# Sigmoid attention with a mixture-of-depths layer: the routed rows as Strassen products of quarters

## Chip, core and metric

The kernel runs on one core of a Trainium2 chip, as one launch, from inputs in DRAM to an output in DRAM. The metric is the device time of the launch in microseconds (us). All arithmetic is in fp32.

## The reference, cut to what matters

```python
# attention: q, k, v are (8, 12, 448, 64)
scores = scale * np.matmul(q, k.transpose(0, 1, 3, 2)) - np.log(S)
attn = 1.0 / (1.0 + np.exp(-scores))
x = np.matmul(attn, v)              # then (B, H, S, D) -> (B, S, H*D): (8, 448, 768)

# mixture of depths: w_gate (768), w1 (768, 1024), w2 (1024, 768), capacity 128
scores = np.einsum('bsd,d->bs', x, w_gate)
out = x.copy()
for b in range(B):
    top_idx = np.argpartition(-scores[b], capacity)[:capacity]
    xe = x[b, top_idx]
    h = np.maximum(xe @ w1, 0.0)
    ye = h @ w2
    g = 1.0 / (1.0 + np.exp(-scores[b, top_idx]))
    out[b, top_idx] = x[b, top_idx] + g[:, None] * ye
```

So each of the 8 sequences sends 128 of its 448 rows through two weight matrices.

## The kernel before, in words

**Attention.** The 96 heads are handled in 24 groups of four (`load`, `turn`), two groups in each of 12 stages s. A stage has seven units n = 0 to 6 (`unit`): 32 score matmuls on TensorE (L213) into two PSUM tiles `psc`, then two sigmoids on ScalarE (L221). `turn(i)` (L188 to L195) transposes the raw q and k rows of group i on VectorE into `qT` and `kT`; groups 2s and 2s+1 are used in stage s, unit 3 needs both. The values of stage s (`values`, L248) are multiplied after unit 6 of stage s and after units 0, 1 and 2 of stage s+1; they fill the PSUM tiles `o`, which four transposes (`take`, L263) empty into `x_b`.

**Loads.** All plain loads and stores stand on the queue of SyncE (SP), in the order of the code: `load` (q and k rows, two buffers each), `load_v` (eight transfers, two buffers), the weight matrices once, near the end of stages 0 and 1, into tiles that stay in SBUF. `store` writes x_b to a DRAM tile `x_d` in four transfers of 128-byte pieces, `copy_out` copies `x_d` to the output.

**Routing.** When a sequence's x is complete, `gate` (DVE) makes its scores; `spread` sends them to DRAM and back as a row on each partition (`rep`), `rank` and `place` count for each row how many are larger, `choose` turns that into 128 row numbers and gathers the rows from `x_d` (GpSimd queue). These steps are `put` at fixed places (stage, unit) and run after the unit by `due`. The small transfers of routing stand on the queue of GpSimd (POOL).

**The routed rows.** `turn_rows` transposes the 128 gathered rows on TensorE (L375). `ffn1` multiplies weights by rows, three blocks of 128 outputs at a time (L391, relu by ScalarE, L394). `ffn2` (L401) multiplies the hidden rows by a third of the second matrix, DVE scales by the gate and adds to the rows (L403), and an indirect DMA scatters them into the output. These pieces wait in the list `ready`; `go` takes one after each of units 3, 4 and 5 from stage 4 on, and the rest after the last stage. They use the tiles `o`, in turn with `psc` at the end.

The order on every engine is the order of the code (`tc.manual_schedule()`); a tile pool makes a new tile wait until the old one in its buffer has been read.

## Time and profile before

| | |
|---|---|
| runs | 472.99 us median of 3 (472.17 to 476.65) |
| profiled execution, its own time | 476.17 us |
| span of the profile | 474.4 us, mean granted clock 0.991 |
| TensorE (PE) busy | 457.4 us (96%) |
| DVE, ACT, POOL busy | 227.3, 184.9, 48.8 us |
| scores L213, values L248 (raw_v), busy | 153.9, 142.2 us |
| routed L391 (tiles o), L401 (tiles o and psc), busy | 69.8, 62.5 and 25.4 us |
| DMA | 72.74 MB, mean 153 GB/s |

In the profile's groups a line such as "L391 PE MATMUL o<-xeT,w_sb ... x576 | 69.8, 281 | ..." reads: line of the kernel, engine, operation, output and inputs, number of instructions, busy time in us, mean ns of one, idle time ahead of it and what ended that. An fp32 matmul is two instructions. The chain of work is followed back from the last instruction; its pieces are start, length and what ran. SPq is SP's queue of DMA issues, raw_k, raw_q and raw_v the tiles of the loads, w_sb both weight matrices. Busy matmuls overlap, so their busy time is not a sum of work.

### The profile page before, as it was taken

To read this page: it belongs to the slowest core of one execution; us is meant where nothing else is said; L and a number is where in the kernel's file an instruction comes from. 1 tells how busy PE (TensorE), PEld (TensorE's weight loads), DVE (VectorE), ACT (ScalarE), POOL (GpSimd) and SP (SyncE) were. 2 spreads that over 40 slices of the span, in tenths; PEclk is the share of its full clock that TensorE was granted. 3 is DMA by queue.
4 is the path that set the end of the run, shared out by engine and by line. 5 is a ranking of instruction groups with operands and counts; after the bars stand their busy time and mean duration, and the time that the engine had idled before them with its cause. 6 is when DMAs were issued, how large, how long until landed. Compare 5 with 4: busy or idle time off the path is not lost.

```text
span 474.4 us, 14579 instructions
## 1 busy us (share of the span) xinstructions
PE 457.4 (96%) x6582; PEld 312.6 (66%) x6582; DVE 227.3 (48%) x559; ACT 184.9 (39%) x245; POOL 48.8 (10%) x76
## 2 busy tenths in 40 slices
PE   8998989897999999999999999999999999999994
PEld 3563635365765684658774666755678738999993
DVE  4309087749140825765710864946254618530100
ACT  4756464544235334435445334445344420101000
POOL 9000000110000011011100011011010010220001
PEclk9999999999899999999999999999999999999999
DMA  8988788799921980985940992985822734722000
GB/s 268 229 324 212 291 196 178 158 262 195 227 70 45 202 202 8 229 177 149 258 171 3 202 202 43 266 153 130 254 69 43 155 83 79 209 57 68 35 0 33
DMA packets 119005, 72.74 MB, mean 153 GB/s; under 512 B 96320, under 2 KB 108800, under 8 KB 118688
## 3 DMA queue, kind: packets, MB, share of 16 engines
q1 hardware_dynamic: 115808, 61.35, 50.8%
q0 software_dynamic: 3136, 10.47, 10.0%
q8 instruction: 51, 0.84, 0.7%
q14 instruction: 10, 0.08, 0.0%
HBM read 57.51 MB, written 25.31 MB: 175 GB/s over the span
## 4 chain that ended last, share of the span: by engine, by line
PE 89%; DMA 4%; DVE 2%; ACT 1%; issue 1%; SPq 0%; POOLq 0%; DVEq 0%; ACTq 0%
PE o L248 25%; PE psc L213 24%; PE o L391 16%; PE o L401 13%; PE psc L401 4%; PE psc L391 3%; PE o L213 2%; DMA raw_h<-in_v_dram 1%; ACT attn L221 1%; DMA scores<-total 1%; DMA rep<-scores 1%; PE o L375 1%; PE o L506 1%; DVE scr L321 1%; DVE scr L318 1%
## 5 line engine op out<-in xcount | busy, mean ns | idle before, releaser
L221 ACT ACTIVATE attn<-psc,bias_s 128x896 f32<-128x896 f32 x156 | 148.6, 1004 | 121.0 <-PE psc L213 120.8
L213 PE MATMUL psc<-qT,kT 32*64 32x448 f32 x2496 | 153.9, 542 | 4.2 <-ACT attn L221 4.2
L248 PE MATMUL o<-attn,raw_v 32*64 32x448 f32 x2304 | 142.2, 540 | 1.1 <-ACT o L251 1.1
L213 PEld LDWEIGHTS psc<-qT,kT 32*64 32x64 f32 x2496 | 66.4, 131 | 57.6 <-issue 33.9
L248 PEld LDWEIGHTS o<-attn,raw_v 32*64 32x64 f32 x2304 | 70.2, 133 | 46.3 <-issue 33.4
L391 PEld LDWEIGHTS o<-xeT,w_sb 128*128 128x128 f32 x576 | 67.2, 196 | 9.8 <-issue 5.7
L263 DVE STREAM_TRANSPOSE x_b<-o 128x448 f32<-128x448 f32 x48 | 26.9, 617 | 97.1 <-PE o L248 97.0
L391 PE MATMUL o<-xeT,w_sb 128*128 128x128 f32 x576 | 69.8, 281 | 0.9 <-ACT xeT L381 0.9
L401 PE MATMUL o<-w_sb,hT 128*128 128x256 f32 x272 | 62.5, 383 | 0.0
L401 PEld LDWEIGHTS o<-w_sb,hT 128*128 128x128 f32 x272 | 50.5, 190 | 14.2 <-issue 4.3
L188 DVE STREAM_TRANSPOSE kT<-raw_k 128x384 f32<-128x384 f32 x48 | 24.7, 552 | 34.2 <-PE psc L213 27.5
L403 DVE SCALAR_TENSOR_TENSOR xe<-o,gate,xe 128x256 f32<-128x256 f32 x17 | 8.2, 483 | 53.4 <-PE o L401 53.3
L318 DVE TENSOR_SCALAR_CACHE_REDUCE scr<-rep,score 128x448 f32<-128x448 f32 (+1 forms) x32 | 21.5, 673 | 20.1 <-DMA rep<-scores 19.2
L274 DVE TENSOR_REDUCE gate_p<-scr 128x14 f32<-128x448 f32 x48 | 29.8, 621 | 1.7
L271 DVE TENSOR_TENSOR scr<-x_b,wg_b 128x448 f32<-128x448 f32 x48 | 29.4, 613 | 1.1
L248 PE MATMUL o<-attn,raw_h 32*64 32x448 f32 x384 | 28.8, 536 | 0.0
L394 ACT ACTIVATE hT<-o 128x384 f32<-128x384 f32 (+1 forms) x20 | 9.1, 453 | 49.5 <-PE o L391 49.5
L401 PE MATMUL psc<-w_sb,hT 128*128 128x256 f32 x112 | 25.4, 380 | 0.0
L195 DVE STREAM_TRANSPOSE qT<-raw_q 128x896 f32<-128x896 f32 x23 | 24.7, 1073 | 1.4 <-DMA raw_q<-in_q_dram 1.4
L401 PEld LDWEIGHTS psc<-w_sb,hT 128*128 128x128 f32 x112 | 21.0, 190 | 3.4 <-issue 0.7
L321 DVE SCALAR_TENSOR_TENSOR scr<-rep,score,earlier 128x448 f32<-128x448 f32 (+1 forms) x32 | 21.8, 683 | 1.4
L298 POOL DMA_DIRECT2D scores<-total x8 | 4.4, 555 | 173.5 <-DVE by_token L300 165.3
(69 smaller groups left out, 222.7 us busy)
## 6 DMA issues: line engine op xcount, KB each, us to landing
raw_k<-in_k_dram SPq DMA_DIRECT2D x24, 448.0 KB, 5.1
raw_q<-in_q_dram SPq DMA_DIRECT2D x24, 448.0 KB, 4.7
x_d<-x_b SPq DMA_DIRECT2D x32, 336.0 KB, 7.6
out_dram<-x_d SPq DMA_DIRECT2D x8, 1344.0 KB, 8.5
raw_v<-in_v_dram SPq DMA_DIRECT2D x48, 192.0 KB, 4.4
w_sb<-in_moe_w_dram SPq DMA_DIRECT2D x6, 512.0 KB, 5.7
w_sb<-in_moe_w_dram SPq DMA_DIRECT2D x8, 384.0 KB, 9.0
spot<-ranks POOLq DMA_DIRECT2D x8, 256.0 KB, 6.2
```

What stands on the lines that cost most here:

```text
L188: nc.vector.transpose(kT[i][:, e, :HK], sk[:, e, :HK].rearrange("p (m c) d -> p c m d", c=NF))
L195: nc.vector.transpose(qT[i], sq)
L213: nc.tensor.matmul(psc[h // 2][y * Dh:(y + 1) * Dh, h % 2, :S], kT[2 * s + x][d, e, r:r + 2, :].rearrange("d r t -> d (r t)"), qT[2 * s + ...
L221: nc.scalar.activation(a, psc[pr][:, :, :S], AF.Sigmoid, bias=bias_s, scale=QK_SCALE)
L248: nc.tensor.matmul(o[x][j * Dh:(j + 1) * Dh, pr, :S], w, a[rows, j, :], start=(n == 0 and c == 0), stop=(n == 3 and c == NF - 1))
L263: nc.vector.transpose(x_tiles[b][:, :, 2 * g + pr, :], outs[s][x][:, pr, :S].rearrange("p (r t) -> p r t", t=TT))
L271: nc.vector.tensor_tensor(out=tmp, in0=x_tiles[b][:, :, hp, :], in1=wg_b[:, hp:hp + 1, :].to_broadcast([P, TB, TT]), op=ALU.mult)
L274: nc.vector.tensor_reduce(out=gate_parts[b][:, :, hp], in_=tmp, axis=AX.X, op=ALU.add)
L318: nc.vector.tensor_scalar(out=junk[:n], in0=rep[:n], scalar1=own, scalar2=0.0, op0=ALU.is_gt, op1=ALU.add, accum_out=above[:n, c:c + 1])
L321: nc.vector.scalar_tensor_tensor(out=junk[:n], in0=rep[:n], scalar=own, in1=earlier[:n, c, :], op0=ALU.is_equal, op1=ALU.mult, accum_out=l ...
L391: nc.tensor.matmul(ps[:, f - f0, :n], w1_sb[:, t, f * P:(f + 1) * P], xeT[:, t // (KD // 2), t % (KD // 2), :n], start=(t == 0), stop=(t = ...
L401: nc.tensor.matmul(ps[:n, :ND], st[b]["hT"][:, t, :n], w2_sb[:, t, cols], start=(t == 0), stop=(t == KF - 1))
```

## The change

Two sequences make a pair; their rows together are a matrix of two row halves, and each weight matrix is cut into quarters. Seven products of quarters by sums of halves take the place of eight (Strassen's scheme in the form with shared sums). For the first matrix, products 1, 2 and 4 use quarters as they are, 3, 5, 6 and 7 use sums of quarters; for the second, 1, 2 and 3 use quarters, 4, 5, 6 and 7 sums.

- `load_weights` loads the quarters; GpSimd makes the eight sums, which are stored in DRAM.
- Three quarters of each matrix stay in SBUF. A sum is loaded when needed (`lend`, on SP) into two attention tiles that are free at that time: after unit 2 of a stage by the table `LENT`, later in `rest`.
- `turn_rows` makes the differences of rows (on DVE for pairs 0 and 3, GpSimd otherwise), `first` and `second` make a product of 12 and 4 matmuls in half of a PSUM tile, `first_sums` and `second_sums` add the products on DVE (and on GpSimd for differences of hidden rows).
- Where each product runs is written out in `WORK` (stage, unit) and `rest`; `ready` and `go` are gone.
- `raw` and `vals` have one buffer. `load(2s+2)` now follows `turn(2s+1)`, `load(2s+3)` follows `turn(2s+2)` at the end of a stage, and `load_v(s)` stands after unit 3 of its own stage. Attention tiles have fixed slots.
- For sequences 2 to 6 the small transfers of routing move from POOL's queue to SP's (`queue`), ahead of the x_d stores; copies to the output move (`routed`).

The core of the diff:

```diff
-    raw = ctx.enter_context(tc.tile_pool(name="raw", bufs=2))
-    vals = ctx.enter_context(tc.tile_pool(name="vals", bufs=2))
+    raw = ctx.enter_context(tc.tile_pool(name="raw", bufs=1))
+    vals = ctx.enter_context(tc.tile_pool(name="vals", bufs=1))
     head = ctx.enter_context(tc.tile_pool(name="head", bufs=2))
-    dram = ctx.enter_context(tc.tile_pool(name="dram", bufs=3, space=bass.MemoryType.DRAM))
+    dram = ctx.enter_context(tc.tile_pool(name="dram", bufs=B, space=bass.MemoryType.DRAM))
...
-        raws[i] = [raw.tile([P, TB * Dh], F32, name=f"raw_{nm}") for nm in "kq"]
+        if i == 1:
+            both = moe.tile([P, 7 * KH * P], F32, name="rows_t")
+            raws[i] = [both[:, n * TB * Dh:(n + 1) * TB * Dh] for n in range(2)]
+        else:
+            raws[i] = [raw.tile([P, TB * Dh], F32, name=f"raw_{nm}") for nm in "kq"]
...
+    def load_weights(m):
+        n = KH if m == 1 else FH
+        w = (w1_sb, w2_sb)[m - 1]
+        held = [(0, 0), (0, 1), (1, 1)] if m == 1 else [(0, 0), (1, 0), (1, 1)]
+        left = (1, 0) if m == 1 else (0, 1)
+        room = moe.tile([P, 7 * FH * P], F32, name="hidden")
+        a, b = room[:, :QW], room[:, QW:2 * QW]
+        c = moe.tile([P, 7 * KH * P], F32, name="rows_t")[:, :QW]
+        for dst, at in [(a, left)] + [(w[:, x], held[x]) for x in (2, 0, 1)]:
+            nc.sync.dma_start(out=dst.rearrange("p (t c) -> p t c", t=n), in_=quarter(m, *at))
+        w00, wx, w11 = [w[:, x] for x in range(3)]
+        def made(key, src):
+            t = sums[m, key] = dram.tile([P, QW], F32, name=f"sum{m}{key}", bufs=1)
+            nc.gpsimd.dma_start(out=t, in_=src)
+        if m == 1:
+            ops = [(5, b, a, w11, ALU.add), (6, c, b, w00, ALU.subtract),
+                   (7, a, w00, a, ALU.subtract), (3, b, wx, c, ALU.subtract)]
+        else:
+            ops = [(5, b, a, w00, ALU.subtract), (6, c, w11, b, ALU.subtract),
+                   (7, a, a, w11, ALU.subtract), (4, b, wx, c, ALU.subtract)]
+        for key, dst, x, y, op in ops:
+            nc.gpsimd.tensor_tensor(out=dst, in0=x, in1=y, op=op)
+            made(key, dst)
+    def attn_tile(pr, slot):
+        return attnp.tile([P, 2, S], F32, name=f"attn{pr}_{slot}")
+    def lend(m, key, slot):
+        halves = []
+        for pr in range(2):
+            t = attn_tile(pr, slot).rearrange("p a s -> p (a s)")[:, :QW // 2]
+            nc.sync.dma_start(out=t, in_=sums[m, key][:, pr * QW // 2:(pr + 1) * QW // 2])
+            halves.append(t)
+        lent[m, key] = halves
...
+            a = attn_tile(pr, f"d{s % 2}{n}" if n < 3 else f"u{n}")
...
+    def queue(b):
+        return nc.gpsimd if b < 2 or b == B - 1 else nc.sync
...
+        nc.scalar.activation(x[:, 2, :, :n], ps[:, 0, :KH, :n], AF.Copy)
+        nc.vector.tensor_copy(x[:, 3, :, :n], ps[:, 1, :KH, :n])
+        eng = nc.vector if p in (0, NP - 1) else nc.gpsimd
+        for dst, y, z in ((4, 2, 0), (2, 3, 2), (5, 3, 4), (6, 1, 5)):
+            eng.tensor_tensor(out=x[:, dst, :, :n], in0=x[:, y, :, :n], in1=x[:, z, :, :n],
+                              op=ALU.subtract)
...
+    ROWS1 = {1: 0, 2: 1, 3: 3, 4: 6, 5: 4, 6: 5, 7: 2}
+    def first(p, key, where="o"):
+        n = CAP
+        x = pairs[p]["x"][:, ROWS1[key]]
+        if key == 1:
+            t = moe.tile([P, 7 * FH * P], F32, name="hidden")
+            pairs[p]["h"] = t.rearrange("p (m k n) -> p m k n", m=7, k=FH)
+        w = weight(1, key)
+        ps = bank(where).rearrange("p (k n) -> p k n", n=P)
+        for f in range(FH):
+            for t in range(KH):
+                nc.tensor.matmul(ps[:, f, :n], w((t * FH + f) * P, P), x[:, t, :n],
+                                 start=(t == 0), stop=(t == KH - 1))
+        return p, key, ps
...
+    def first_sums(p, key, ps):
+        n = CAP
+        h = [pairs[p]["h"][:, m, :, :n] for m in range(7)]
+        ps = ps[:, :FH, :n]
+        def add(dst, a, b):
+            nc.vector.tensor_tensor(out=dst, in0=a, in1=b, op=ALU.add)
+        def relu(t):
+            nc.scalar.activation(t, t, AF.Relu)
+        if key == 1:
+            nc.scalar.activation(h[2], ps, AF.Copy)
+        elif key == 2:
+            add(h[0], ps, h[2])
+            relu(h[0])
+        elif key == 6:
+            add(h[2], ps, h[2])
...
+            if p == NP - 1:
+                nc.vector.scalar_tensor_tensor(out=h[4], in0=h[2], scalar=0.0, in1=h[3],
+                                               op0=ALU.max, op1=ALU.add)
+                nc.vector.tensor_tensor(out=h[5], in0=h[4], in1=h[0], op=ALU.subtract)
+                nc.vector.scalar_tensor_tensor(out=h[2], in0=h[2], scalar=0.0, in1=h[0],
+                                               op0=ALU.max, op1=ALU.subtract)
+                nc.vector.tensor_tensor(out=h[6], in0=h[1], in1=h[5], op=ALU.subtract)
+                return
+            relu(h[2])
+            for dst, a, b, op in ((4, 2, 3, ALU.add), (5, 4, 0, ALU.subtract),
+                                  (2, 2, 0, ALU.subtract), (6, 1, 5, ALU.subtract)):
+                nc.gpsimd.tensor_tensor(out=h[dst], in0=h[a], in1=h[b], op=op)
...
+    ROWS2 = {1: 0, 2: 1, 3: 6, 4: 3, 5: 4, 6: 5, 7: 2}
+    QUARTERS = {1: ((0, 0), (0, 1), (1, 0), (1, 1)), 2: ((0, 0),), 3: ((0, 1),), 4: ((1, 0),),
+                5: ((1, 1), (0, 1)), 6: ((0, 1), (1, 0), (1, 1)), 7: ((1, 1), (1, 0))}
+    def second(p, key, where="o"):
+        n = CAP
+        h = pairs[p]["h"][:, ROWS2[key]]
+        w = weight(2, key)
+        ps = bank(where)
+        for t in range(FH):
+            nc.tensor.matmul(ps[:n, :DH], h[:, t, :n], w(t * DH, DH),
+                             start=(t == 0), stop=(t == FH - 1))
+        return p, key, ps
+    def second_sums(p, key, ps):
+        n = CAP
+        left = pairs[p].setdefault("left", {q: 4 if q[0] or q[1] else 2 for q in QUARTERS[1]})
+        for x, m in QUARTERS[key]:
+            b = 2 * p + x
+            cols = slice(m * DH, (m + 1) * DH)
+            xe = st[b]["xe"]
+            nc.vector.scalar_tensor_tensor(
+                out=xe[:n, cols], in0=ps[:n, :DH], scalar=st[b]["gate"][:n, 0:1],
+                in1=xe[:n, cols], op0=ALU.mult, op1=ALU.add)
+            left[x, m] -= 1
+            if p == NP - 1 and not left[x, m]:
+                scatter(b, m)
...
+    WORK = {
+        (4, 3): [("t", 0)], (4, 4): [(1, 0, 1)], (4, 5): [(1, 0, 2)],
+        (5, 3): [("t", 1)], (5, 4): [(1, 0, 7), (1, 0, 6)], (5, 5): [(1, 0, 4)],
+        (6, 3): [(2, 0, 1), (2, 0, 2)], (6, 4): [(1, 0, 5)], (6, 5): [(1, 0, 3), (2, 0, 4)],
+        (7, 3): [(2, 0, 3)], (7, 4): [(2, 0, 5)], (7, 5): [(2, 0, 6), (2, 0, 7), ("s", 0)],
+        (8, 3): [("t", 2), ("t", 3), (1, 1, 1)], (8, 4): [(1, 1, 2)],
+        (8, 5): [(1, 1, 7), (1, 1, 6)],
+        (9, 3): [(1, 1, 4)], (9, 4): [(1, 1, 5)], (9, 5): [(1, 1, 3), (2, 1, 1)],
+        (10, 3): [(2, 1, 2)], (10, 4): [(2, 1, 4), (2, 1, 5)], (10, 5): [(2, 1, 6)],
+        (11, 3): [(2, 1, 3)], (11, 4): [(2, 1, 7), ("s", 1)],
+        (11, 5): [("t", 4), ("t", 5), (1, 2, 1), (1, 2, 2)],
+    }
+    LENT = {5: [(1, 7), (1, 6)], 6: [(1, 5), (1, 3), (2, 4)], 7: [(2, 5), (2, 6), (2, 7)],
+            8: [(1, 7), (1, 6)], 9: [(1, 5), (1, 3)], 10: [(2, 4), (2, 5), (2, 6)],
+            11: [(2, 7), (1, 7), (1, 6)]}
...
+        put(s, 4, spread, b)
+        put(s, 4, store, b)
+        put(s + 1, 1, ranking, b)
         if s + 2 <= NS:
-            put(late, *((s + 1, 6) if b == 0 else (s + 2, 0)), choose, b)
-            put(late, s + 2, 3, follow, b)
+            put(*((s + 2, 1) if b % 2 else (s + 1, 5)), copy_out, b)
+            put(s + 2, 0, choose, b)
...
+                for i, (m, key) in enumerate(LENT.get(s, ())):
+                    lend(m, key, f"d{(s + 1) % 2}{i}")
...
+    def rest():
+        for n in range(3):
+            gap(NS, n)
+        room = [f"d1{i}" for i in range(3)] + [f"u{n}" for n in range(3, NU)] + ["d00"]
+        for key in ((1, 5), (1, 3)):
+            lend(*key, room.pop(0))
+        p, b = NP - 2, B - 1
+        work = [(item, begin(item, "any")) for item in ((1, p, 6), (1, p, 7))]
+        gates(2 * NS - 1)
+        st[b]["x_d"] = None
+        store(b)
+        gate(waiting.pop())
+        for key in ((2, 4), (2, 5), (2, 6), (2, 7), (1, 7)):
+            lend(*key, room.pop(0))
+        for item, args in work:
+            finish(item, args)
+        spread(b)
+        for key in (4, 5, 3):
+            do((1, p, key), "any")
+        lend(1, 6, "d01")
+        ranking(b)
+        choose(b - 1)
+        for key in (1, 2, 3, 4, 5, 6):
+            do((2, p, key), "any")
+        for key, slot in (((1, 5), "d02"), ((1, 3), "d10")):
+            lend(*key, slot)
+        choose(b)
+        do((2, p, 7), "any")
+        do(("s", p))
+        copy_out(b - 1)
+        copy_out(b)
+        p += 1
+        for item in (("t", b - 1), (1, p, 1), (1, p, 2), ("t", b)):
+            do(item, "any")
+        for key, slot in (((2, 6), "d11"), ((2, 5), "d12"), ((2, 7), "u3"), ((2, 4), "u4")):
+            lend(*key, slot)
+        for key in (7, 6, 4, 5, 3):
+            do((1, p, key), "any")
+        for key in (1, 2, 6, 5, 7, 3, 4):
+            do((2, p, key), "any")
...
                     turn(2 * s + 1)
-                    load(2 * s + 3)
-                if n == 0:
-                    load_v(s + 1)
+                    if s > 0:
+                        load(2 * s + 2)
+                if n == 3 and s > 0:
+                    load_v(s)
                 gap(s, n)
                 if n == NU - 2:
                     turn(2 * s + 2)
-                    load(2 * s + 4)
-                load_weights(*WEIGHTS.get((s, n), (0, 0)))
-        for n in range(5):
-            gap(NS, n)
-        go("any")
-        choose(B - 2)
-        while len(ready) > 3:
-            go("any")
-        ranking(B - 1)
-        copy_out(B - 1)
-        while len(ready) > 1:
-            go("any")
-        follow(B - 2, "any")
-        for n in range(2):
-            go("any")
-        choose(B - 1)
-        while len(ready) > 1:
-            go("any")
-        follow(B - 1, "any")
-        while ready:
-            go("any")
-        assert not late
+                    load(2 * s + 3)
+                if n == NU - 2 and s < 2:
+                    load_weights(s + 1)
```

## The prediction, made before the changed kernel was run

> **What bounds the kernel now.** I read the page first: engines, the chain that ended last, the costliest groups.
>
> ```profile
> span 474.4 us, 14579 instructions
> ...
> PE 457.4 (96%) x6582; PEld 312.6 (66%) x6582; DVE 227.3 (48%) x559; ACT 184.9 (39%) x245; POOL 48.8 (10%) x76
> ...
> DMA  8988788799921980985940992985822734722000
> ...
> PE 89%; DMA 4%; DVE 2%; ACT 1%; issue 1%; SPq 0%; POOLq 0%; DVEq 0%; ACTq 0%
> ...
> L391 PE MATMUL o<-xeT,w_sb 128*128 128x128 f32 x576 | 69.8, 281 | 0.9 <-ACT xeT L381 0.9
> ...
> L401 PE MATMUL o<-w_sb,hT 128*128 128x256 f32 x272 | 62.5, 383 | 0.0
> ```
>
> PE is 89% of the chain, so PE work removed counts, as long as nothing new makes PE wait. The routed products (L391, L401) are on that chain. DMA works in bursts: nine tenths in many slices, nothing in others.
>
> Next the chain in order of time, one stage of the attention loop (the values of s=8 end at 294.3; I call that moment T9, and so on):
>
> ```profile
> 295.86 4.25 PE o L391 x36
> 300.12 1.69 PE psc L213 x32
> 301.80 4.22 PE o L391 x36
> 306.02 1.69 PE psc L213 x32
> 307.71 2.88 PE o L391 x24
> ```
>
> 36 matmuls take 4.22, 24 take 2.88; on L401, 16 take 3.65. T9 to T10 (327.3) is 33.0, of which routed work is 11.35: 21.7 is left for scores and values. Then SP's timeline from the same moment, and DVE's ranking:
>
> ```profile
> 299.52 0.38 SPq L95 DMA_DIRECT2D raw_k<-in_k_dram  x1
> ...
> 300.46 0.53 SPq L283 DMA_DIRECT2D out_dram<-x_d  x1
> 301.18 16.71 SPq L280 DMA_DIRECT2D x_d<-x_b  x4
> 317.98 2.76 SPq L95 DMA_DIRECT2D raw_k<-in_k_dram  x1
> 320.84 0.38 SPq L95 DMA_DIRECT2D raw_q<-in_q_dram  x1
> ```
>
> ```profile
> 281.87 0.64 DVE L318 TENSOR_SCALAR_CACHE_REDUCE scr<-rep,score 128x448 f32<-128x448 f32 x1
> ...
> 287.81 0.21 DVE L329 STREAM_TRANSPOSE by_col<-place_s 128x32 f32<-128x32 f32 x1
> ```
>
> The four stores of x_d hold SP's queue for 16.7, because it fills and drains in order: the q and k rows behind them are issued at 318 and 320.8 and land at about 324.7 (4.6 median for raw_q), 30.4 after T9. Here that costs nothing: they are for the transposes near the end of the next stage. The waits of DVE say so:
>
> ```profile
> DVE kT L188 <- DMA raw_k<-in_k_dram: 3.1, 2, 2.7
> ...
> DVE qT L195 <- DMA raw_q<-in_q_dram: 1.4, 2, 0.7
> ```
>
> **The change, part by part.**
>
> *Products.* Each pair has 7 first products of 24 instructions (12 matmuls, two passes) and 7 second ones of 8 with 384 columns; four pairs make 28 and 28, instead of 768 and 384 instructions. A first one is the 24-group above, 2.88 (2.68 in the tail); a second one is 3.65 x 8/16 x 384/256 = 2.74 (2.60). Inside the loop the table of work has 16 first, 14 second and six row transposes of 0.66: 46.1 + 38.4 + 4 = 88.4. Before, from T4 (110.8, plus 3.7 of waiting on DVE) to the end of the values at 392.2, eight intervals less 8 x 21.7 leave about 104. Gain: 15.7.
>
> *The tail.* Before, PE runs from 392.2 to 467.4 without a gap: 75.2. After it has 12 x 2.68 + 14 x 2.60 + 1.3 = 69.9. But the last pair needs both sequences chosen before its third product, and the chain of the last sequence (scores out, rep back, ranking, spot, gather) lies as before: rep at +17.6, ranking to +24, spot landing about +33, gather about +40. I count 0.5 of waiting at the first gather, 2.4 after the second one for its copies and differences, 1.8 for GpSimd's four hidden sums before product 3, so PE ends at about +75.4. Nothing is gained; bounds -5 (no wait) to +4.
>
> *Additions on DVE and ACT.* 8 additions of 512 columns and 14 of 384 per pair, at the rates of L271 (613 ns for 448) and L403 (483 for 256): about 14 per pair, 56 in all, less 11.6 for the old L403. DVE rises to some 280 of 500: room. Cover: PE has four o banks as halves, and the sums trail a product by 0.7 to 1.4. Without cover it is up to 0.7 per product; I take 0.
>
> *Sums of weights on GpSimd.* Eight operations of 1536 columns. Nearest rows: 553 ns for a cast of 448 (1.9 scaled) and 1395 for L172 (4.8). With w1 landed near 28 and stores between, w2 can load from 41 to 52, and the scores of sequence 0, queued on POOL behind them, leave between 60 and 82; rep is back 8 later, ranking needs it at 80. Cost 0 to 10; I take 2, in between.
> The Trainium skill (GPSIMD Engine Reference, section 3.1) gives 4497 ns for a two-input add of 2048 columns; an estimate by it is 3.4 each, and the sum would be 0 for this term.
>
> *Weights from DRAM.* 32 loans of 786 KB. Packets of 3072 bytes (the second matrix's load) took 132 ns on 16 queues: 2.1 per loan, 67 in all, and 18 for the stores of sums. Engines were 61% busy, 292; they come to 377. As a mean that fits; the order on SP doesn't.
>
> *One buffer for q/k rows and v.* This decides. The load for transpose 2s+3 now stands behind turn(2s+2), at the end of stage s, so on SP behind: loans, v, scores, rep (which waits for scores to land), four x_d stores and in stages 6 and 9 a copy to out as well. In the next stage's order on DVE, turn(2s+3) comes before the ranking, and that before the four transposes that free the o banks. So a late row makes PE wait at unit 3 (kT) or at the first routed product (o).
> Row first: with two buffers DVE waited 4.5 in all for these rows. The Trainium skill (Trainium Kernel Development and Optimization, Best Practices) asks for double buffering so that DMA overlaps compute, which speaks against this part; taken with the row of before, the term would be nothing, taken with the rule, what follows.
>
> From T: a loan 2.1, v 4.8 (SP's 8 issues at 260.8 to 264.5 landed at 266.6), scores landing +2, rep +0.7; from the x_d issue to the rows' landing 16.9 (301.18 to 324.7 is 23.5, less 2.9 for rows and 3.7 for the copy ahead); a copy 3.7. After landing: turn 2.2, ranking 5.9 to 6.2, two transposes 1.1; PE can cover 1.7 of that with unit 3.
>
> - Stages 5 and 8 (two loans): landing at T+30.5. T6 is T5+33.5 (21.7 + 9.3 + 2.5), T9 is T8+35. Waits 4.7 and 3.2: take 5 and 3.
> - Stage 6 (three loans, which now leave only after the ranking's ranks and spot, at +8, packets from +11): v has landed at +23, landing of rows 46; stage length 41: 12.9. Stage 9: 42 against 38.8: 10.9. Take 13 and 11.
> - Stage 3 (no loans, scores on POOL, a copy): 26.5 against 26, so ranking ends 6 later than at 113.3. Take 6.
>
> Sum 38. Best case, loans and v leaving at T with no push by the ranking: 3.6 + 2.1 + 7.7 + 7.7 + 3 = 24. Worst, with late loans in full: 54.
> Small ones: stages 4 and 5 have only a transpose between two units, ACT needs 1.9 for a unit's two tiles: 1.3 each, 2.6. In stages 7, 9, 10 the second item needs a loan that comes up to 3.5 late (0 to 3.5 each); I take 4 together.
>
> Sum against the profiled span: 474.4 - 15.7 + 0.2 + 2 + 38 + 2.6 + 4 = 505.5. Its own time was 476.17, 1.8 above the span: 507.3. The median of the runs (472.99) is 0.67% lower: 504.
>
> **Rivals.**
> *The rows come in time* (faster). If x_d, copy and rows drained side by side, so that rows land 7.7 before T (turn and ranking done by then), only the products count: 474.4 - 15.5 = 458.9, or 457.5 by the median. For: DMA stands at 0 in 5 of 40 slices, PE's interval of 33 to 36 is about what SP's chain takes. Against: 16.7 in one SP row, and the order on DVE. It decides from a total of waits under 15.5.
> *Only the bare wait* (slower, small): loans leave at T, waits 24 and no small ones: 483 span, 481 by the median. For: PE's own stretching gives SP time. Against: ranks and spot stand ahead of the loans.
> *Everything late* (slower, large): 54 for the rows and loans, GpSimd's upper end of 10: 523 span, 521. For: one late stage pushes the next. Against: stages 8 and 11 have no ranking and let SP catch up.
> That the products aren't fewer is excluded: the program's order has 56 products.
>
> **How the numbers follow.** Rows late, 504: 0.60, own range 490 to 515. Bare wait 0.12; everything late 0.10; rows in time 0.14; 0.04 near no change, where part of the waits cancels the gain. The range goes from 474, which leaves out rows in time and part of no change, to 524. A change under 1% can't be told from none here. Faster 0.14, same 0.04, slower 0.82.
>
> **What would show it.** Right: DVE's waits for raw_k and raw_q of tens of us, in stages 4, 6, 7, 9, 10, PE's idle time ahead of L213 and of the first routed product, x_d stores on SP followed by rows that land after T; routed products at 2.9 and 2.7; GpSimd sums between 1.9 and 4.8. Wrong: PE busy at 9 in all slices with a span near 460, rows landing before the values end; or waits at the loans (PE waiting for the lent tiles), not at the rows.

## Result and profile after

| | before | after |
|---|---|---|
| median of the runs | 474.82 us (472.17 to 478.45, 4 runs) | 552.68 us (551.53 to 556.21, 4 runs) |
| profiled execution, span, mean granted clock | 476.17, 474.4, 0.991 | 556.21, 554.2, 0.944 |
| T12 (end of the values of the last stage) | 392.2 | 445.9 |
| from T12 to the last matmul | 75.1 | 101.6 |
| PE without work before its last matmul | 8.5 | 80.5 |

After is 1.163 times before (95% interval 1.154 to 1.173). Medians here and below are over all executions, while a ratio and its interval leave out the few that were in a slower state of the chip. The forecast was 504, range 474 to 524: the direction was right, the size was not. The page of after, its head and two groups:

```profile
span 554.2 us, 14369 instructions
...
PE 465.5 (84%) x6326; PEld 273.7 (49%) x6326; DVE 293.8 (53%) x637; ACT 184.6 (33%) x240; POOL 92.5 (17%) x92
...
PEclk9999987896999988997999998998999997799998
...
L533 PE MATMUL o<-w_sb,hidden 128*128 128x384 f32 x72 | 34.9, 645 | 25.9 <-DVE x_b L319 15.6
...
L474 PE MATMUL o<-rows_t,attn_d 128*128 128x128 f32 x264 | 36.0, 300 | 10.2 <-DVE hidden L484 5.7
```

The routed products now stand behind 26 and 10 us of idle time. PE was 0.9 idle ahead of L391 before and not at all ahead of L401 in `o`. PEclk falls to 6 and 7 in slices where PE waits. The list of waits (engine, line, waited for: us in total, times, longest) names four sorts:

```profile
DVE kT L244 <- DMA raw_k<-in_k_dram: 44.2, 9, 12.9
...
PE o L533 <- DVE x_b L319: 15.6, 3, 5.6
PE o L533 <- DVE xe L544: 13.4, 5, 6.3
...
PE psc L269 <- DVE qT L251: 12.9, 4, 9.2
```

The first two are the late rows that the prediction spoke of: DVE's wait for raw_k is 44.2 instead of 3.1. SP's timeline and DVE's around T10 (368.0) show the steps in the order in which they were forecast:

```profile
346.09 9.03 SPq L336 DMA_DIRECT2D x_d<-x_b  x4
355.16 2.95 SPq L339 DMA_DIRECT2D out_dram<-x_d  x1
358.20 1.45 SPq L100 DMA_DIRECT2D raw_k<-in_k_dram  x1
```

```profile
366.57 1.04 DVE L244 STREAM_TRANSPOSE kT<-raw_k 128x384 f32<-128x384 f32 x2 [10.41 <-PE o L304]
...
374.83 2.24 DVE L319 STREAM_TRANSPOSE x_b<-o 128x448 f32<-128x448 f32 x4
```

x_d, the copy, the rows; then on DVE the turn of the rows, the ranking (368.7 to 374.8), and only then the transposes that free `o`. The view puts DVE's 10.41 down to PE, but raw_k landed at 366.5 (358.20 plus 8.3 from issue to landing), 0.1 ahead of the turn. So this wait too is one for late rows, and the 44.2 is a lower bound. PE's first routed product of stage 10 waits 5.6.

The other two sorts were not in the prediction. The 9.2 is the wait of unit 0 of stage 3 for `qT`. PE waits from 74.0 to 83.1. Here is what DVE does ahead of the turn that makes this `qT`, and GpSimd beside it:

```profile
65.07 3.65 DVE L327 TENSOR_TENSOR scr<-x_b,wg_b 128x448 f32<-128x448 f32 x1
68.75 0.62 DVE L330 TENSOR_REDUCE gate_p<-scr 128x14 f32<-128x448 f32 x1
...
70.00 6.92 DVE L353 COPY parts<-by_dim 32x32 f32<-32x32 f32 x4
```

```profile
64.78 3.45 POOL L166 TENSOR_TENSOR rows_t<-w_sb,hidden 128x1536 f32<-128x1536 f32 x1
...
69.10 3.45 POOL L166 TENSOR_TENSOR hidden<-hidden,w_sb 128x1536 f32<-128x1536 f32 x1
...
73.44 3.43 POOL L166 TENSOR_TENSOR hidden<-w_sb,rows_t 128x1536 f32<-128x1536 f32 x1
```

While GpSimd makes the second matrix's sums, a product on DVE that takes 0.58 to 0.63 with no sum beside it takes 3.65, and four small copies that take 0.72 take 6.92. The reduction between them keeps its 0.62.

The last sort is in the tail: second products of pair 2, and what DVE does just ahead of the one that comes late.

```profile
470.57 2.74 PE L533 MATMUL o<-w_sb,hidden 128*128 128x384 f32 x8
479.63 4.18 PE L533 MATMUL o<-w_sb,hidden 128*128 128x384 f32 x6 [6.32 <-DVE xe L544]
```

```profile
476.77 2.18 DVE L544 SCALAR_TENSOR_TENSOR xe<-psc,gate,xe 128x384 f32<-128x384 f32 x4
478.87 0.61 DVE L544 SCALAR_TENSOR_TENSOR xe<-o,gate,xe 128x384 f32<-128x384 f32 x1
```

The product at 479.63 goes into the free half of a tile `o`. It starts 0.15 after DVE has read the product in the other half (478.87 plus 0.61), and that reading stood behind the ranking. GpSimd's last hidden sum had ended at 475.2. So by the trace this product waited for the reader of the other half of its PSUM tile, not for its inputs; the run with a tile for each product tests that.

### The profile page after: what moved, and what is told of

It reads as the page before. It is cut to its first block, busy times and chain, and to the rows that moved or that the text cites. A ratio compares the mean times of both kernels' runs of the same rounds, so it can differ in the third digit from the quotient of the medians.

```text
span 554.2 us, 14369 instructions
## 1 busy us (share of the span) xinstructions
PE 465.5 (84%) x6326; PEld 273.7 (49%) x6326; DVE 293.8 (53%) x637; ACT 184.6 (33%) x240; POOL 92.5 (17%) x92
## 5 line engine op out<-in xcount | busy, mean ns | idle before, releaser
L269 PE MATMUL psc<-qT,kT 32*64 32x448 f32 x2496 | 161.0, 553 | 17.3 <-DVE qT L251 12.9
L304 PE MATMUL o<-attn_d,raw_v 32*64 32x448 f32 x1152 | 131.1, 541 | 0.6 <-ACT o L307 0.3
L304 PE MATMUL o<-attn_u,raw_v 32*64 32x448 f32 x1152 | 127.0, 540 | 1.4 <-ACT o L307 0.8
L277 ACT ACTIVATE attn_u<-psc,bias_s 128x896 f32<-128x896 f32 x86 | 81.9, 1004 | 121.4 <-PE psc L269 121.3
L277 ACT ACTIVATE attn_d<-psc,bias_s 128x896 f32<-128x896 f32 x70 | 66.7, 1004 | 57.8 <-PE psc L269 57.7
L304 PEld LDWEIGHTS o<-attn_u,raw_v 32*64 32x64 f32 x1152 | 51.3, 133 | 30.4 <-issue 21.0
L244 DVE STREAM_TRANSPOSE kT<-raw_k 128x384 f32<-128x384 f32 x46 | 23.8, 555 | 73.6 <-DMA raw_k<-in_k_dram 44.2
L304 PEld LDWEIGHTS o<-attn_d,raw_v 32*64 32x64 f32 x1152 | 50.2, 133 | 21.2 <-issue 18.9
L533 PE MATMUL o<-w_sb,hidden 128*128 128x384 f32 x72 | 34.9, 645 | 25.9 <-DVE x_b L319 15.6
L474 PE MATMUL o<-rows_t,attn_d 128*128 128x128 f32 x264 | 36.0, 300 | 10.2 <-DVE hidden L484 5.7
L474 PEld LDWEIGHTS o<-rows_t,attn_d 128*128 128x128 f32 x264 | 34.2, 213 | 15.0 <-DVE hidden L484 6.7
L533 PEld LDWEIGHTS o<-w_sb,hidden 128*128 128x128 f32 x72 | 17.3, 251 | 42.2 <-issue 34.1
L327 DVE TENSOR_TENSOR scr<-x_b,wg_b 128x448 f32<-128x448 f32 x48 | 36.5, 761 | 1.0
L474 PE MATMUL o<-rows_t,w_sb 128*128 128x128 f32 x264 | 32.3, 279 | 3.4 <-ACT rows_t L451 1.9
L474 PEld LDWEIGHTS o<-rows_t,w_sb 128*128 128x128 f32 x264 | 30.3, 192 | 8.2 <-issue 3.1
```

Of the source, the lines that this page charges most:

```text
L244: nc.vector.transpose(kT[i][:, e, :HK], sk[:, e, :HK].rearrange("p (m c) d -> p c m d", c=NF))
L269: nc.tensor.matmul(psc[h // 2][y * Dh:(y + 1) * Dh, h % 2, :S], kT[2 * s + x][d, e, r:r + 2, :].rearrange("d r t -> d (r t)"), qT[2 * s + ...
L277: nc.scalar.activation(a, psc[pr][:, :, :S], AF.Sigmoid, bias=bias_s, scale=QK_SCALE)
L304: nc.tensor.matmul(o[x][j * Dh:(j + 1) * Dh, pr, :S], w, a[rows, j, :], start=(n == 0 and c == 0), stop=(n == 3 and c == NF - 1))
L327: nc.vector.tensor_tensor(out=tmp, in0=x_tiles[b][:, :, hp, :], in1=wg_b[:, hp:hp + 1, :].to_broadcast([P, TB, TT]), op=ALU.mult)
L474: nc.tensor.matmul(ps[:, f, :n], w((t * FH + f) * P, P), x[:, t, :n], start=(t == 0), stop=(t == KH - 1))
```

## Experiments

Each kernel was timed beside the kernel before on the same chip; T12 and "tail" (T12 to the last matmul) are from the profiled execution. Diffs are against after unless said.

**One part alone.**

*The stores of x_d two units later.*
```diff
-        put(s, 4, store, b)
+        put(s, 6, store, b)
...
-            put(*((s + 2, 1) if b % 2 else (s + 1, 5)), copy_out, b)
+            put(*((s + 2, 1) if b % 2 else (s + 1, 6)), copy_out, b)
```


> Theory A (the rows are late because they stand behind the four x_d stores on SP): with the stores and the copy moved two units later, behind the loads of rows, PE's waits at the first routed product in stages 4, 6, 7 and 10 (5.1, 4.4, 5.6 and 5.6 us, together 20.7) go, and with them the half-clock stretches that follow them (some 10 us); DVE's wait for raw_k falls from 44.2 to under 10. I expect 520 to 535 us against 552.7. Rival B (the DMA engines are full anyway, whatever the order on SP): the rows land as late as now, 545 to 556. Both: the waits of the tail stay, and the wait of 9.2 in stage 3 stays.

556.46, ratio 1.166 (1.150 to 1.181): no gain. DVE's wait for raw_k did fall, from 44.2 to 24.8, but now the loans stand behind the stores: PE waits 9.8, 11.0 and 6.8 for `attn_d<-sum`, where it waited 3.3 and 3.2 in all. Rival B's time, for a reason that neither theory named: a wait changes its place when SP's order does.

*A PSUM tile for each product.*
```diff
-        if half[0] is None:
-            half[0] = banks(where)
-            return half[0][:, 0]
-        t, half[0] = half[0], None
-        return t[:, 1]
+        return banks(where)[:, 0]
```


> Each product gets a PSUM tile of its own instead of half of one. Theory A (a product in the second half of a tile waits until DVE has read the first half's product, because the wait is made for the tile): the waits at tiles read by the sums, 4.8, 6.3, 1.8, 1.2 and a dozen of 0.7 to 0.9 in the tail and 2.3, 1.8 in the loop, together about 22, shrink, and the half-clock stretches of the tail with them: 530 to 540 us. Rival B (the sums stand on DVE behind gates and ranking, and the products need them as inputs or for the buffer anyway): the waits move to other products, 545 to 556.

539.65, 1.130 (1.115 to 1.145). As theory A has it: 13 less; the tail goes from 101.6 to 88.2. Of the tail's 10.0 of idle time that is left, the longest piece (3.6) is ahead of the transposes of sequence 6's rows.

*The small sums on DVE.*
```diff
-        eng = nc.vector if p in (0, NP - 1) else nc.gpsimd
+        eng = nc.vector
...
-                nc.gpsimd.tensor_tensor(out=h[dst], in0=h[a], in1=h[b], op=op)
+                nc.vector.tensor_tensor(out=h[dst], in0=h[a], in1=h[b], op=op)
```


> The row differences of pairs 1 and 2 and the hidden sums of pairs 0 to 2 made on DVE instead of GpSimd; the eight sums of weights stay on GpSimd. Theory A (only the long sums of weights matter, the small ones lie beside other work): 548 to 557 us. Rival B (every two-input operation of GpSimd holds DVE up, and the small ones too): DVE's sums behind them get shorter and the time falls by about 10, 540 to 545.

556.57, 1.171 (1.162 to 1.179). Theory A.

*No sums of weights.*
```diff
-            nc.gpsimd.tensor_tensor(out=dst, in0=x, in1=y, op=op)
-            made(key, dst)
+            made(key, a)
```


> Leaves out the eight additions of weight quarters on GpSimd: a plain quarter is stored in DRAM in place of each sum, with the same transfers, so the products use other weights. Theory A (while GpSimd adds two tiles, DVE stands still: the copies of L353 took 6.9 instead of 0.7 us and one operation of L327 3.65 instead of 0.6): the turn of stage 3's rows comes in time, the wait of 9.2 ahead of unit 3 of stage 3 goes and so does most of the 10.2 us at half clock behind it: 537 to 543 us. Rival B (the rows of that stage are late through the transfers of the sums and of x_d): the wait stays within 2 us of 9.2, 549 to 556.

550.19, 1.155 (1.144 to 1.167): rival B's range, and the 2.5 less than after are within the intervals. (The text says unit 3 of stage 3; the wait is ahead of unit 0 of that stage.) DVE's copies and products are back:

```profile
66.18 0.63 DVE L326 TENSOR_TENSOR scr<-x_b,wg_b 128x448 f32<-128x448 f32 x1
...
68.09 0.72 DVE L352 COPY parts<-by_dim 32x32 f32<-32x32 f32 x4
```

The 9.2 is gone and T2 to T3 takes 27.6 instead of 37.1. But T3 to T4 takes 35.7 instead of 27.9, with PE waiting 1.9 for the turn and 4.2 for x_b, after DVE has waited 15.6 for raw_k: the chain of late rows, a stage earlier. So the mechanism of theory A is shown, and its price is not: 7.8 of the 9.5 are given back in the next stage.

*Sums of weights in eight pieces.* (`QW` is 1536.)
```diff
-            nc.gpsimd.tensor_tensor(out=dst, in0=x, in1=y, op=op)
+            for o in range(0, QW, QW // 8):
+                nc.gpsimd.tensor_tensor(out=dst[:, o:o + QW // 8], in0=x[:, o:o + QW // 8],
+                                        in1=y[:, o:o + QW // 8], op=op)
```


> Each sum of weights on GpSimd is made in eight pieces of 192 columns instead of one operation of 1536. Theory A (DVE is held for as long as one GpSimd operation lasts): DVE's copies of L353 and the operations of L327 wait at most 0.5 us each, the turn for stage 3 comes in time and the wait of 9.2 shrinks to under 3; a part comes back in stage 4, as without the sums: 546 to 552. Rival B (DVE and GpSimd share the port for the whole time, pieces or not): the wait stays within 2 us of 9.2: 551 to 557.

558.59, 1.169 (1.159 to 1.179). DVE's four copies take 1.97 beside the pieces, where they took 6.92, and T2 to T3 takes 28.0, as theory A says; T3 to T4 takes 42.2, so nothing is won, and the time is over both ranges. A sum in pieces lasts 4.4 to 5.6 instead of 3.4, and what is queued behind it on GpSimd is later.

*No loans.*
```diff
     def lend(m, key, slot):
+        return
...
-        x = {(1, 1): 0, (1, 2): 1, (1, 4): 2, (2, 1): 0, (2, 2): 1, (2, 3): 2}[m, key]
+        x = {(1, 1): 0, (1, 2): 1, (1, 4): 2, (2, 1): 0, (2, 2): 1, (2, 3): 2}.get((m, key), 0)
```


> Leaves out all 32 loans: every product that would use a lent sum uses a resident quarter instead, so SP issues no loans and the DMA engines move 25 MB less; products, sums on DVE and everything else stay. Theory A (SP's queue is the pacer: v, scores, x_d stores and rows stand behind the loans, each loan 2.1 us): the loop's waits for rows and loans in stages 6, 7, 9 and 10 (4.4, 5.6, 3.0, 5.6 and 1.7, with the half-clock stretches behind them some 30 us) go, stages 4 and the tail stay: 518 to 530. Rival B (one buffer alone is enough to make rows late, loans or not): half of it stays, 535 to 548.

543.52, 1.134 (1.122 to 1.147): rival B, nine less. DVE's wait for raw_k stays, at 50.7.

*Two buffers.*
```diff
-    raw = ctx.enter_context(tc.tile_pool(name="raw", bufs=1))
-    vals = ctx.enter_context(tc.tile_pool(name="vals", bufs=1))
+    raw = ctx.enter_context(tc.tile_pool(name="raw", bufs=2))
+    vals = ctx.enter_context(tc.tile_pool(name="vals", bufs=2))
...
-                    if s > 0:
-                        load(2 * s + 2)
-                if n == 3 and s > 0:
-                    load_v(s)
+                    load(2 * s + 3)
+                if n == 0:
+                    load_v(s + 1)
...
-                    load(2 * s + 3)
+                    load(2 * s + 4)
```


> Two buffers for q and k rows and for v again, with the loads where the kernel before had them; the room is made by leaving out one resident quarter of each weight matrix (its products and sums use another quarter; two loads of 0.8 MB are not made). Loans, stores and products stay. Theory A (the prediction's: one buffer makes the rows late, so that DVE and then PE wait): DVE's wait for raw_k falls from 44.2 to under 10, PE's waits for x_b in stages 4, 6, 7, 10 go with their half-clock stretches; the tail stays: 510 to 525. Rival B (the DMA engines or SP's queue are too slow for loans and rows together, whatever the buffers): 540 to 553.

575.29, 1.206 (1.194 to 1.217): 23 slower than after, which neither theory allowed. Rows are in time (3.5 in all), loans are not. Its SP timeline in stage 7 and a line of its waits:

```profile
249.88 1.81 SPq L115 DMA_DIRECT2D raw_v<-in_v_dram  x4
...
253.72 0.37 SPq L96 DMA_DIRECT2D raw_k<-in_k_dram  x1
...
259.29 0.38 SPq L389 DMA_DIRECT2D spot<-ranks  x1
259.76 4.69 SPq L173 DMA_DIRECT2D attn_d<-sum  x6
```

```profile
PE o L529 <- DMA attn_d<-sum: 21.8, 2, 11.1
```

*Two buffers, loans first.* Against the last one:
```diff
-                    load(2 * s + 3)
-                if n == 0:
-                    load_v(s + 1)
+                if n == (0 if s == 0 else 3):
+                    load_v(s + 1)
+                    load(2 * s + 3)
```


> Two buffers as in the earlier run (one quarter of each matrix left out), but v and the rows of the next stage are issued after unit 3, behind the loans, instead of after units 0 and 1, ahead of them. Theory A (the earlier run's 575 came from the order: loans stood behind v, which waits on SP until the old values are done, and behind rows; with loans first both are in time): 505 to 530. Rival B (rows, v, loans and x_d don't fit into a stage in any order): 545 to 575.

522.67, 1.096 (1.092 to 1.101): theory A, 30 less than after, T12 413.6. The same buffers, the same transfers, 53 us apart by the order on one queue; in stage 7 the loans left at 233.4, T7 being 233.3, and 10.0 after T7 (249.8) in the run before.

```profile
233.39 4.74 SPq L173 DMA_DIRECT2D attn_d<-sum  x6
```

*Loans on GpSimd's queue.*
```diff
-            nc.sync.dma_start(out=t, in_=sums[m, key][:, pr * QW // 2:(pr + 1) * QW // 2])
+            nc.gpsimd.dma_start(out=t, in_=sums[m, key][:, pr * QW // 2:(pr + 1) * QW // 2])
```


> The loans are issued on GpSimd's queue instead of SP's; nothing else is changed and no work is left out. Theory A (what costs is that v, stores and rows stand behind the loans on one queue): as without loans or nearly, 540 to 547. Rival B (the loans cost as traffic on the shared DMA engines, whatever the queue; or they become late themselves): 549 to 562.

556.70, 1.167 (1.161 to 1.173): rival B's range. Rows with one buffer are late all the same: DVE waits 52.8 for raw_k.

*Work for PE ahead of its waits.*
```diff
...
+        if (s, n) in ((4, 3), (6, 3), (7, 3), (10, 3)):
+            keep_warm([banks("psc"), banks("psc")], 2 * s + 1, 32)
         for item in WORK.get((s, n), ()):
```


> Adds matmuls whose results nobody reads just ahead of five waits of PE: 64 before unit 3 of stage 3, 32 each before the first routed item of stages 4, 6, 7 and 10 (about 6.8 and 3.4 us of work at full clock). Theory A (a wait of PE of 3 us or more is followed by stretches at half clock, which cost as much again): the stretches behind these five waits (10.2, 10.2, 3.4, 6.8 and 3.4 us) go or shrink, and although work was added the time falls by 6 to 14: 539 to 547. Rival B (the half clock has another cause, such as heat or power, and comes anyway): 552 to 560.

564.75, 1.186 (1.177 to 1.195), over both ranges. One of the five places was chosen wrongly (unit 3 of stage 3 doesn't wait, unit 0 does): the 64 matmuls there are pure loss, and T3 to T4 grew by 8.2. The other four tell something. Stage 6, first of after and then of this run (start and end, length, busy us by engine, PEclk, DMA share, GB/s):

```profile
198.00:246.00 48.00, 39.79 (x533) 21.13 (x526) 24.58 (x61) 15.19 (x20) 6.00 (x5) 0.93 0.66 174
```

```profile
201.00:251.00 50.00, 45.70 (x639) 26.24 (x622) 25.77 (x61) 16.82 (x22) 5.99 (x5) 1.00 0.67 169
```

The clock stays at 1.00, so in these stages the half clock does come from PE's waits. But stage 4 takes 36.5 instead of 38.7, stage 6 47.4 instead of 47.8, stage 7 44.7 instead of 46.1 and stage 10 44.0 as before. (Stage 9, where nothing was added, takes 43.5 instead of 39.9: its wait for a loan is 4.7 instead of 3.0.) So PE's speed is not what sets the length of these four stages; the late rows fit, and the runs with two buffers bear it out.

**Costs taken away one after the other.**

*Two buffers and no loans* (both diffs above).


> Leaves out the 32 loans (a resident quarter in place of each) and has two buffers for q, k rows and v with the loads where the kernel before had them (one quarter of each matrix left out for the room). Theory A (rows and v are late because one buffer and the loans together leave SP no time; either alone is not enough to cure it): the waits of stages 4, 6, 7, 9 and 10 go, T12 falls from 445.9 to 390 to 405, the tail of 101 stays: 495 to 512. Rival B (the x_d stores, or the DMA engines, pace the loop by themselves): 525 to 545.

513.99, 1.079 (1.075 to 1.084), a little over theory A's range. T12 402.7, as theory A has it. T1 to T3 takes 66.0 where the kernel before takes 49.7: here the sums of weights show.

*The same with a tile for each product.*


> The run without loans and with two buffers (513.99 us), and a PSUM tile for each product besides; the sums of weights on GpSimd stay. It splits the 44 us that lie between that run and the products alone (469.75). Theory A (the tail's 24 us are the shared tiles, the loop's 21 us the sums of weights, which come out in full once the rows are in time): T12 stays near 400 and the tail falls from 102 to 78 to 82, 488 to 493. Rival B (the shared tiles cost in the loop as well, the sums of weights little, as the 2.5 us of leaving them out alone would say): T12 falls under 390 too, 470 to 482.

483.72, 1.015 (1.008 to 1.023), between the theories: the tail (79.8) is as theory A has it, T12 (394.6) lies between. So the shared tiles cost 22 in the tail and 8 in the loop. At the place in the tail where after waited 6.32 for DVE, PE waits 2.63 for a hidden sum of GpSimd:

```profile
416.26 2.85 PE L520 MATMUL o<-w_sb,hidden 128*128 128x384 f32 x8 [2.63 <-POOL hidden L506]
```

*The same without sums of weights.*


> All suspected costs taken away at once, so that little more than the seven products and their sums is left: no loans, two buffers, a PSUM tile for each product, and no sums of weights on GpSimd (a plain quarter stored instead); weights and results differ. Theory A (these four are all that is lost; the products are worth what the prediction gave them): T12 near 380 to 388 and a tail of 88 as in the run with a tile of its own for each product, 470 to 482. Rival B (something else in the change costs as well, such as the order on DVE or GpSimd's other work): over 490.

469.75, 0.986 (0.980 to 0.992), a little under theory A's range: T12 381.6, tail 78.2, clock 0.989. With the sums, PE waited 4.6 and 6.5 for `qT` ahead of unit 0 of stages 2 and 3; these two waits are gone. So no other large cost is hidden in the change.

**With nothing left out.** Five kernels with a tile for each product, two buffers for rows only (x_b in four thirds makes the room), loans ahead of v and rows, and sums in pieces. From the second on, each diff shows part of what changed against the one before it.

```diff
-            x_tiles[b] = rows_p.tile([P, TB, HP, TT], F32, name="x_b")
+            x_tiles[b, g] = rows_p.tile([P, TB, 2, TT], F32, name="x_b", bufs=4)
...
-        return nc.gpsimd if b < 2 or b == B - 1 else nc.sync
+        return nc.gpsimd
...
+                if n == (1 if s == 0 else 3):
+                    load(2 * s + 3)
...
-                    load(2 * s + 3)
+                    load(2 * s + 4)
```


> Nothing left out: a PSUM tile for each product; two buffers for q and k rows (the room comes from holding x_b in four thirds instead of two wholes); loans ahead of v and rows on SP; ranks, spot and scores of every sequence on GpSimd's queue; the copies to the output in stages 4, 7 and 10, which store no x_d; sums of weights in pieces of 384 columns, those of the second matrix a stage later. Theory A (each loss has been found, and none but the tail's 8 to 10 us of late loans and late rows stays): T12 at 383 to 393, tail 80 to 88, 470 to 486, so near the kernel before or a little slower. Rival B (loans, v and stores together still make PE wait in stages 6, 7 and 10): 490 to 510.

504.22, 1.062 (1.055 to 1.070): rival B's range, but not for its reason. The intervals from T5 to T12 are 34.3, 35.4, 32.6, 36.5, 33.7, 32.9 and 33.0, the very numbers of the run with two buffers, no loans and a tile for each product: with loans first and rows early, the loans cost the loop nothing. T3 to T4 takes 49.3, for one wait, which runs through four engines:

```profile
118.95 0.77 POOL L394 DMA_DIRECT2D spot<-ranks  x1 [5.71 <-DMA ranks<-by_col]
```

```profile
126.57 0.69 DVE L406 SCALAR_TENSOR_TENSOR scr<-spot,slot,number 128x448 f32<-128x448 f32 x1 [21.39 <-DMA spot<-ranks]
```

```profile
128.02 0.20 ACT L421 ACTIVATE gate<-got 128x1 f32<-128x1 f32 x1 [17.64 <-DVE scr L406]
```

The ranks stand behind the sums on GpSimd's queue (they leave at 112.7, right after the last sum), spot behind the ranks, DVE waits for spot, the gate on ACT for DVE, and the next sigmoids (128.1) stand behind the gate. PE waits 15.3 ahead of unit 2 of stage 4.

```diff
-                if n == NU - 2 and s in (0, 2):
-                    load_weights(1 if s == 0 else 2)
+                if n == NU - 2 and s < 2:
+                    load_weights(s + 1)
...
-        for key in ((2, 4), (2, 5), (2, 6), (2, 7), (1, 7)):
+        for key in ((2, 4), (2, 5), (2, 6)):
...
-        for key in (7, 6, 4, 5, 3):
-            do((1, p, key), "any")
+        third = begin((1, p, 3), "any")
```


> The last run (504.22 us) with two changes of order, nothing left out. First: sums of weights in pieces of 192 columns, those of the second matrix where they stood before (end of stage 1), and the small transfers of sequence 0 on SP, so that its spot doesn't stand on GpSimd's queue behind the sums; that should take away the wait of 15.3 in stage 4 and its half clock. Second, in the tail: lent sums stay in their tiles for the last pair (5 loans there instead of 13), the choice of sequence 6 is made ahead of the ranking of sequence 7, and the last pair's third first product starts before the products that wait for row differences. Theory A (only that one wait and the tail's crowd were left): T12 at 381 to 385 instead of 406.7, tail 75 to 80 instead of 86, 464 to 474, so faster than the kernel before. Rival B (the weight sums in stages 1 to 3 hold the x_d stores and rows in any order, and another wait takes the place of the 15.3): T12 over 392, 478 to 495.

487.24, 1.022 (1.016 to 1.027). The tail is 78.2, as expected. The loop is rival B: the 15.3 became waits of 1.3, 3.0, 1.1 and 4.6, and T3 to T4 still takes 40.5.

```diff
+        if m == 2:
+            yield
         for key, dst, x, y, op in ops:
...
+        do((2, p, 1), "any")
         ranking(b)
-        for key in (1, 2, 3, 4, 5, 6):
+        for key in (2, 4, 5, 6, 3):
             do((2, p, key), "any")
```


> Nothing left out; against the last run (487.24 us) only order is changed. Start: the second matrix is loaded at the end of stage 1 as there, but its sums are issued on GpSimd at the end of stage 2, behind the scores and rep of sequence 0, which go back to GpSimd's queue, so that v isn't held on SP behind spot; ranking of sequence 0 one unit later. Tail: five loans ahead of the last x_d store, one second product's sums ahead of the last ranking, the product that needs GpSimd's last hidden sum after the others, row transposes of the last pair one product earlier. Theory A (the 14 us in the stage after T3 are waits for rep and v in the queues, the 5.9 of the tail are waits on GpSimd's sums, ACT and row differences): T12 at 383 to 388, tail 71 to 75, 463 to 472. Rival B (the DMA engines are full in stages 2 and 3 with both weight loads, their sums and two x_d, whatever the queue): T12 stays over 394, 476 to 486.

480.05, 1.012 (1.006 to 1.019): the time is in rival B's range, T12 (391.5) between the theories, T3 to T4 33.8. The tail is 76.4, with one wait of 3.5 for a copy on ACT behind a gate.

```diff
-        put(s, 4, store, b)
+            put(s, 4, store, 2 * s - 2)
+            put(s, 4, store, 2 * s - 1)
...
-        choose(b)
         do(("t", b - 1), "any")
+        choose(b)
         do((2, p, 7), "any")
```


> Nothing left out; against the last run (480.05 us): each third of a sequence's x is stored to x_d in the stage after it is finished instead of all three with the last one, the copies to the output are spread over stages 4, 5, 6, 8, 9 and 10, the second matrix's resident quarters are loaded ahead of the quarter that waits for room, its sums are issued in two halves around the scores of sequence 0; in the tail the rows of sequence 6 are transposed before the choice of sequence 7, whose gate on ScalarE held their copy for 3.5. Theory A (what is left in stages 3 and 4, 9 us, and in the tail, 4 us, is DMA traffic in bursts and that order on ScalarE): T12 at 382 to 387 instead of 391.5, tail 71 to 75 instead of 76.4, 463 to 473. Rival B (the even traffic collides with the loans in stages 6 to 11, where nothing waits now): new waits there, 476 to 490.

484.43, 1.014 (1.010 to 1.019), in rival B's range. The tail (72.9) is shorter than before's 75.1 and of the intervals from T5 on two grew, by 1.3 each, so rival B's collision is small. But T2 to T4 takes 65.4, since the second matrix's last quarter landed at 71 and the scores of sequence 0 waited behind its sums until 82.

```diff
-                if (s, n) in ((2, 0), (2, 5)):
+                if (s, n) in ((2, 5), (3, 4)):
```


> Nothing left out; against the last run (484.43 us) only the place of the second matrix's four sums on GpSimd's queue is changed: two at the end of stage 2, behind scores and rep of sequence 0, two in stage 3 behind those of sequence 1, so that no small transfer of routing stands behind more than two of them. Theory A (the last run's 14 us in stages 2 and 3 are scores held on that queue until 82, since the sums ahead of them waited for their quarter until 71): T4 at 112 to 117 instead of 124.9, all else as there: 470 to 477. Rival B (DMA traffic of weights, sums and stores in these stages): T4 over 121, 480 to 487.

480.90, 1.012 (1.007 to 1.017): the time is in rival B's range. T4 comes at 117.3, near theory A, and then the rows of sequence 0 are late: their gather stands behind the last sum, and PE waits 8.2 for them.

```profile
112.31 6.05 POOL L165 TENSOR_TENSOR hidden<-w_sb,rows_t 128x192 f32<-128x192 f32 x8
119.67 1.05 POOL L428 DMA_INDIRECT xe<-x_d,row  x1 [0.45 <-DMA raw_v<-in_v_dram]
```

T5 is 156.5 against 142.7 in the run of the products alone: all that separates the two loops lies ahead of it. No version with nothing left out that beats the kernel before was found. Without these 13.8 the span would be 465, an estimate from the two runs; a place for eight sums and their 12.6 MB of loads and stores ahead of T5 stays open.

## Why the prediction was right or wrong

The chain of runs, each with one cost less, beside the terms of the sum (us, medians):

| step | measured | forecast |
|---|---|---|
| after to two buffers and loans first (552.68 to 522.67) | 30.0 | together 38 for rows and 4 for loans |
| no loans (to 513.99) | 8.7 | |
| a tile for each product (to 483.72) | 30.3 | 0 |
| no sums of weights (to 469.75) | 14.0 | 2 |
| what is left against before (476.59 beside it) | -6.8 | -15.7 + 2.6 + 0.2 = -12.9 |

The steps depend on their order: alone, a tile for each product is worth 13.0 and the sums of weights 2.5 (not clear of the noise), because another wait stood in the same stretch. The step without loans also puts the loads of rows and v back to their places in the kernel before. The last row leaves 6 of the forecast gain unaccounted for, 3 of them in the tail (78.2 against 75.1 before).

*Products*: right. First ones took 2.84 to 2.94 (2.88 forecast), second ones 2.74 to 2.85 (2.74). T12 of the products alone is 381.6, where 392.2 - 15.7 + 2.6 gives 379.1.

*Late rows*: right in mechanism and near in size, 38.7 against 42, though the two terms divide otherwise: with two buffers and loans first, leaving the loans out still gains 8.7. The waits themselves are shorter than forecast (5.6 instead of 11 in stage 10, 6.4 instead of 13 in stage 7), and what follows them runs at half clock. By length, stages 7 and 10 are 13.3 and 11.1 longer than in the products alone, but stages 4, 6 and 9 are 9.2, 12.1 and 6.2 longer where 6, 5 and 3 of waiting were forecast; shared tiles and loans are in these too. The Trainium skill ("Trainium Kernel Development and Optimization", Best Practices) asks for double buffering, and the prediction weighed that. The runs agree only with the loads in the right order: 522.67 with them behind the loans, 575.29 ahead of them.

*The tail*: wrong, and the largest error. "PE has four o banks as halves, and the sums trail a product by 0.7 to 1.4 ... I take 0" is the step that failed, and the "0.2" of the sum stood on it. Halves are not independent here: the product in one half waits until DVE has read the other, and that cost 30.3 once rows and loans were out of the way, 22 of it in the tail. Also the sums do not trail by 0.7 to 1.4 there: in the tail they stand behind gates, ranking and choosing, 9 us without a break (467.8 to 476.9). Measured 101.6 against 75.4 forecast, and 79.8 with a tile for each product, two buffers and no loans. The waits listed were counted from data alone; who else reads the tile was not asked.

Some sums of the prediction do not come out as written. The tail's terms, 69.9, 0.5, 2.4 and 1.8, add up to 74.6, not 75.4. The 260.8 to 266.6 quoted for v are 5.8, not 4.8. The terms for the rows of stage 5 give a landing at T+28.6, not 30.5, and those of stage 6 less one loan give 44 for stage 9, not 42. These are 1 to 2 each, small beside the 48.7 by which the forecast missed.

*Sums of weights on GpSimd*: the 3.4 was right (3.43 to 3.46), the effect was not. The step looked only at GpSimd's queue (the scores behind the sums, 0 to 10). It left out that DVE's two-input operations and copies wait meanwhile. The Trainium skill ("SBUF — State Buffer", section "Who interferes with whom") says it: a GpSimd operation and a DVE operation with two SBUF inputs, or one in a two-port mode, shut each other out for a whole instruction. The trace agrees: two-input operations and copies stretched from 0.6 to 3.65 and from 0.72 to 6.92, the reduction kept its 0.62. The price came out at 14.0, over the bound of 10, and only once the rows were in time.

*Additions on DVE*: its load (293.8 of 554) is near the 280 of 500 forecast; the cover failed at the tiles, which the sums empty.

*Half clock*: no term of the prediction. PE ran about 42 us at half clock in after, so some 21 us of its speed were lost (estimate: half of it). In four stages of the loop that cost little, as the run with added work shows; in the tail, where PE ran 10.5 us at half clock, about 5 (estimate: half of it).

The rivals: "rows in time" is the products alone with a tail that waits, 469.75 against 457.5; in after the rows were late. "Only the bare wait" (481) is far off. "Everything late" (521) came nearest, in part by luck: its 54 for rows and loans is over the 38.7 of the chain, its 10 for GpSimd is under the 14.0, and it has nothing for the shared tiles.

## What to carry to other kernels

For every tile that a new instruction writes, ask who must have read it before and what stands ahead of that reader on its own engine; a half of a PSUM tile was not a buffer of its own here. A second buffer helps only with the place of its load on the queue: put the transfer that is needed first and can't leave early at the head, and what can be fetched a stage ahead behind it. When several waits overlap, take the costs away one on top of the other; one at a time, most of them look free.

## What was not expected of the hardware

- Four copies of 32 x 32 took 6.92 instead of 0.72 beside GpSimd sums of 1536 columns (3.4 each), and 1.94 to 1.97 beside sums of 192 columns; transposes (0.20 to 0.21) and reductions (0.62) beside them were not touched.
- The length of one wait of PE does not tell whether half clock follows. In the run of the products alone none was granted after a wait of 2.98, and 3.4 us were after one of 1.40 (from 44.2 on); in after 3.4 us were granted after one of 2.99. In after 10.2 us began within the wait of 9.2, and another 10.2 after a wait of 2.1, before the one of 5.1 began. The rule of the Trainium skill ("TensorE: Matmul & The Clock Gate", "HAM oscillation — how this bites in real kernels"), no idle gaps over about 3.4 us, was not enough here: shorter gaps were followed by half clock too.
- A sum of 1536 columns in eight pieces took 4.4 to 6.1 on GpSimd instead of 3.4.
